# A chunked linear recurrence and two feed-forward layers on one core: other PSUM banks, score masks and state sums for the first attentions

## The chip, the cores and the metric

One core of one Trainium2 chip runs the whole kernel as a single launch. The time is device microseconds of one execution; the kernel before takes 1198.31 us (median of 3 runs, 1196.89 to 1199.21). The engines are named as the profile names them: PE (TensorE), with PEld for its weight loads, DVE (VectorE), ACT (ScalarE), POOL (GpSimd) and SP (the queue that starts most transfers).

## The reference, cut to what matters

A gated recurrence over 768 steps for 4 batches of 8 heads of width 48, with a complex decay per step, then two dense feed-forward layers on the 3072 resulting rows.

```python
def attention(q, k, v, a_re, a_im):             # B, H, S, D = 4, 8, 768, 48
    mag = sqrt(a_re**2 + a_im**2)
    scale = minimum(mag, 0.999) / (mag + 1e-6)
    ar, ai = a_re * scale, a_im * scale
    for t in range(S):
        S_re, S_im = ar[t] * S_re - ai[t] * S_im, ar[t] * S_im + ai[t] * S_re
        S_re = S_re + outer(k[t], v[t])
        y[t] = q[t] @ S_re

x = y as [3072, 384]
h = x @ w_in1;  x = (h * clip(h + 3, 0, 6) / 6) @ w_out1            # d_ff = 2048
h = x @ w_in2;  out = (max(h, 0) + alpha * min(h, 0)) @ w_out2
```

## The kernel before, in words

**Attention.** The 768 steps of a batch are cut into six chunks of 128 steps (C). A *group* n is two chunks of one batch, so there are 12 groups, three per batch. For each group VectorE and ScalarE norm the decays (`norm_ops`), and take their running products over the steps (`scan_ops`): local products over 8 steps, then totals of 16 blocks that PE transposes (`totals`, line 408, tile `ptt`), four doubling rounds, the *turn* that a chunk hands to the next (`phi`), and the products E, transposed back by PE (`back`, line 489, tile `pe`). From these come Kt and, in A, Qt (line 518): keys and queries with the decays folded in. `chunk_ops` is then the attention of one chunk g of the group. `tr` (line 563) transposes Kt and Qt by PE, four blocks at a time, into a PSUM tile `pt`, and ScalarE copies that to KT and QT. In the copy the output's access order puts neighbouring elements J = 8 elements apart. `scores(i)` makes 4 heads' scores in the PSUM tile `ps`, and VectorE multiplies them by the causal mask into PT (line 590). `outputs` (line 619) multiplies PT by v and, behind the first chunk, QT by the state W, into `py`; ScalarE copies `py` to ys, and six small transfers bring it into xr, the feed-forward's input. `update` (line 594) adds keys times values (`pu`) to W and scales W by the chunk's decay (`gx`). For groups below WACT = 4 the scaling is eight ScalarE instructions (line 614). KN, the keys in their natural order, comes by eight transfers per chunk.

**Feed-forward.** `ffn(layer, groups, ...)` runs one *pass*: layer 1 or 2 on one group (256 columns, a *single pass*) or on two groups (512 columns, a *pair pass*). Its 16 steps i have `ain` (9 products into `ph`), `gate` and `bout` (9 products into three accumulators `acc`). Every product of float32 numbers is three products of fp32r halves. The order of passes: layer 1 of group 0 (pass 0), layer 1 of group 1 (pass 1), layer 2 of both (pass 2), the same for groups 2 and 3, then pairs for the rest. `split_x` makes the halves xT of a group's input: a cast by ScalarE, a difference by VectorE.

**Weights.** They come as 64-bit floats. `decode_f64` and `split_w` turn a tile into two fp32r halves by four VectorE instructions, two of ScalarE and a difference on VectorE; that is done once per tile, in the passes that use it first, and the tiles stay in 15 places of SBUF or go out to a scratch buffer and come back.

**PSUM.** It has eight banks: two for `ph` (pool psh), one each for `pt` (also `ptt`, `pe`, `gx`), `ps` (also `pu`) and `py`, and three for acc0, acc1 and acc2.

**What sets the order.** A timeline gives each piece of work a position by hand (`group(...)` from line 732, `passes`), and pieces are issued in that order. A scheduler then orders each engine's queue by its own estimates and by priority, which falls in the order of issue. Each engine runs its queue strictly in order and waits at its head.

## Time and profile before

| what | value |
|---|---|
| median of 3 runs | 1198.31 us |
| the profiled execution | 1198.93 us |
| its span, from first to last instruction | 1197.2 us |
| busy PE, DVE, ACT, POOL | 1031.2, 802.1, 615.3, 2.0 us |
| mean granted TensorE clock | 0.975 |

The stages, by PE's rows: until 78 us norms, scan of group 0 and decoding of weights; attention 0 from 78.25 us; pass 0 at full rate from 121.61; attention 1 from 169.08; pass 1 from 210.67; pass 2 from 248.68 with attention 2 among its products; passes of layer 1 for groups 2 and 3 from 337.89 and 404.45, with attention 3 among the first; from 480 us pair passes of layers 1 and 2 in turn, each with the attention of later groups among its products.

How to read the rows: a group of instructions has its line, engine, operation, tiles (out<-in), forms and count, then its busy time and the mean time of one, then the idle time of the engine before them with the releaser. A wait names engine, tile and line on the left, and on the right what ended the wait. Times in windows are counted from the span's start.

### The profile page before, as it was taken

The page shows a single profiled execution, that of the slowest core. Times are in us where ns is not written, and L with a number is a line of the kernel's source. Part 1 is how long each engine was busy: PE and PEld are TensorE (multiplying, and loading weights), DVE is VectorE, ACT ScalarE, POOL GpSimd, SP SyncE. Part 2 cuts the span into 40 slices and gives each one's busy share as a digit, 9 for nine tenths or more (in the row PEclk, how much of TensorE's full clock was granted, in tenths as well). Part 3 has the DMA queues.
Part 4 walks back from the last instruction along what each step waited for, and adds up shares of the span by engine and source line. Part 5 has one row for each costly group of instructions (what it writes and reads, how often), then busy time and mean ns, then how long its engine had stood idle before and what let it go on. Part 6 is the DMA issues. An engine that isn't in the chain of part 4 may idle for free.

```text
span 1197.2 us, 15796 instructions
## 1 busy us (share of the span) xinstructions
PE 1031.2 (86%) x5914; PEld 846.9 (71%) x5914; DVE 802.1 (67%) x1537; ACT 615.3 (51%) x1003; POOL 2.0 (0%) x13
## 2 busy tenths in 40 slices
PE   0026946979998789999999999999999999999997
PEld 0015935957787787777878778778788777788786
DVE  7985973999895586948738749559579375333432
ACT  5453634667665455755356564446554346432433
POOL 0000000000000000000000000000000000000000
PEclk9999876999999899999999999999999999999999
DMA  8642472476575675445534544543454344244430
GB/s 339 253 167 61 142 303 67 134 275 194 222 247 181 213 243 178 134 128 174 171 102 153 171 120 158 193 136 116 131 188 139 130 124 138 89 163 134 133 129 30
DMA packets 70500, 194.60 MB, mean 163 GB/s; under 512 B 29456, under 2 KB 38672, under 8 KB 70416
## 3 DMA queue, kind: packets, MB, share of 16 engines
q1 hardware_dynamic: 70272, 193.50, 48.6%
q8 instruction: 49, 0.80, 0.3%
q14 instruction: 35, 0.29, 0.1%
q10 hardware_dynamic: 144, 0.01, 0.0%
HBM read 158.08 MB, written 22.81 MB: 151 GB/s over the span
## 4 chain that ended last, share of the span: by engine, by line
PE 66%; DVE 16%; ACT 12%; DMA 3%; issue 2%; SPq 0%; DVEq 0%; ACTq 0%
PE ph L658 27%; PE acc L695 24%; PE ps L589 5%; PE pt L566 4%; ACT KT L567 4%; ACT QT L567 4%; PE pu L599 3%; PE py L624 2%; DVE w L294 2%; DVE wd L76 2%; DVE wd L77 2%; PE py L626 2%; DMA w<-wsd 1%; DVE gs L680 1%; DMA A<-in_al_dram 1%
## 5 line engine op out<-in xcount | busy, mean ns | idle before, releaser
L695 PE MATMUL acc<-gs,w 128*128 128x512 f32 (+1 forms) x2016 | 453.3, 366 | 7.2 <-ACT gs L679 4.8
L695 PEld LDWEIGHTS acc<-gs,w 128*128 128x128 f32 x2016 | 335.2, 188 | 69.2 <-ACT gs L679 7.3
L658 PE MATMUL ph<-xT,w 128*128 128x256 f32 (+1 forms) x1152 | 231.2, 348 | 20.9 <-ACT xT L550 14.9
L658 PE MATMUL ph<-xs,w 128*128 128x512 f32 x864 | 224.3, 401 | 3.2 <-DVE xs L704 2.5
L658 PEld LDWEIGHTS ph<-xT,w 128*128 128x128 f32 x1152 | 185.1, 197 | 50.8 <-ACT xT L550 16.0
L658 PEld LDWEIGHTS ph<-xs,w 128*128 128x128 f32 x864 | 158.3, 188 | 40.6 <-DVE xs L704 4.0
L679 ACT CAST gs<-r 128x512 fp32r<-128x512 f32 x192 | 119.7, 624 | 119.6 <-DVE r L671 71.6
L680 DVE TENSOR_TENSOR gs<-r,gs 128x512 fp32r<-128x512 f32 x192 | 132.0, 689 | 63.5 <-ACT gs L679 63.4
L678 DVE SCALAR_TENSOR_TENSOR r<-n,nal,r 128x512 f32<-128x512 f32 x96 | 71.9, 749 | 80.9 <-ACT n L675 80.5
L670 ACT ACTIVATE r<-ph 128x512 f32<-128x512 f32 x96 | 57.3, 597 | 129.2 <-PE ph L658 128.7
L671 DVE SCALAR_TENSOR_TENSOR r<-r,ph 128x512 f32<-128x512 f32 x96 | 65.7, 684 | 83.4 <-ACT r L670 82.9
L674 ACT ACTIVATE r<-ph 128x512 f32<-128x512 f32 x96 | 57.5, 599 | 83.9 <-PE ph L658 83.1
L567 ACT COPY KT<-pt 96x512 f32<-96x512 f32 x48 | 54.8, 1143 | 47.6 <-PE pt L566 39.4
L590 DVE TENSOR_TENSOR PT<-ps,mask 128x512 f32<-128x512 f32 x48 | 33.2, 692 | 62.7 <-PE ps L589 61.0
L589 PEld LDWEIGHTS ps<-QT,KT 96*128 96x128 f32 x384 | 54.5, 214 | 21.8 <-ACT QT L567 18.5
L589 PE MATMUL ps<-QT,KT 96*128 96x128 f32 x384 | 60.5, 307 | 10.7 <-ACT QT L567 9.7
L567 ACT COPY QT<-pt 96x512 f32<-96x512 f32 x48 | 54.8, 1142 | 21.5 <-PE pt L566 21.5
L566 PE MATMUL pt<-ident,Kt 128*96 128x128 f32 x192 | 33.1, 298 | 38.0 <-DVE Kt L518 30.5
L675 ACT ACTIVATE n<-ph 128x512 f32<-128x512 f32 x96 | 57.4, 598 | 0.0
L566 PEld LDWEIGHTS pt<-ident,Kt 128*96 128x96 f32 x192 | 22.6, 136 | 48.6 <-ACT wd L73 21.2
L566 PE MATMUL pt<-ident,A 128*96 128x128 f32 x192 | 33.8, 303 | 20.9 <-ACT QT L567 10.3
L566 PEld LDWEIGHTS pt<-ident,A 128*96 128x96 f32 x192 | 20.9, 135 | 38.7 <-ACT QT L567 19.0
(107 smaller groups left out, 1054.0 us busy)
## 6 DMA issues: line engine op xcount, KB each, us to landing
w<-wsd SPq DMA_DIRECT2D x139, 768.0 KB, 4.4
raw<-in_w_dram SPq DMA_DIRECT2D x32, 768.0 KB, 5.7
wsd<-w SPq DMA_DIRECT2D x23, 768.0 KB, 4.1
A<-in_al_dram SPq DMA_DIRECT2D x12, 768.0 KB, 4.6
qk<-in_qkl_dram SPq DMA_DIRECT2D x12, 768.0 KB, 5.4
KN<-Kt SPq DMA_DIRECT2D x160, 48.0 KB, 2.3
v<-in_vl_dram SPq DMA_DIRECT2D x12, 384.0 KB, 4.4
out_dram<-o SPq DMA_DIRECT2D x18, 256.0 KB, 3.2
```

The source lines that it names most:

```text
L566: nc.tensor.transpose(pt[:D2, jj], src[:, 4 * half + jj, g].rearrange("p c d -> p (c d)"), ident)
L567: nc.scalar.copy(dst.rearrange("p h (t j) -> p j (h t)", j=J)[:, 4 * half : 4 * half + 4], pt[:D2])
L589: nc.tensor.matmul(ps[:, hh], lhsT=KTr[:, h], rhs=QT[:, h], start=True, stop=True)
L658: nc.tensor.matmul(ph_, lhsT=w[:, wl, kk], rhs=x[:, xl, kk], start=(kk == 0 and wl == 0 and xl == 0), stop=(kk == KT - 1 and wl == 1),)
L670: nc.scalar.activation(r, ph_, AF.Relu, bias=0.5, scale=1.0 / 6.0)
L671: nc.vector.scalar_tensor_tensor(r, r, 1.0, ph_, op0=ALU.min, op1=ALU.mult)
L674: nc.scalar.activation(r, ph_, AF.Relu)
L675: nc.scalar.activation(neg, ph_, AF.Relu, scale=-1.0)
L678: nc.vector.scalar_tensor_tensor(r[:, k], neg[:, k], nal[:, ii : ii + 1], r[:, k], op0=ALU.mult, op1=ALU.add)
L679: nc.scalar.copy(gs[:, 0], r)
L680: nc.vector.tensor_sub(gs[:, 1], r, gs[:, 0].bitcast(F32))
L695: nc.tensor.matmul(acc, lhsT=w[:, wl, e * P : (e + 1) * P], rhs=gs[:, gl], start=(i == 0 and wl == 0 and gl == 0), stop=(i == NF - 1 and g ...
```

## The change

- *Banks for the turn.* `totals` and `back` of groups 0 to 2 use the bank acc2 instead of `pt`. That bank is free because a single pass now has its three accumulators in two banks: one alone (acc1), two as halves of acc0. A product of zeros opens acc0, the two halves accumulate behind it, and their last step hands them on together.
- *Turns ahead.* `totals` and `back` of groups 0 to 3 are issued with a priority raised by 1000, so the scheduler puts them further ahead.
- *Banks for attentions 0 and 1.* Every second `pt` and the second `ps` of a chunk use a `ph` bank.
- *Copies of KT and QT, in all groups.* The copy now walks the output in runs of four neighbouring elements, and the PSUM input in steps of 128 elements.
- *Scores of groups 0 to 3.* ScalarE copies them to PT and GpSimd's affine_select zeroes what lies above the diagonal, in place.
- *State of groups 0 to 3.* W is added to `pu` by a product with the identity, and the eight scalings read PSUM. `gx` lies in the bank of `pu` in all groups.

```diff
+URGE = 1000
...
+    zero = cp.tile([1, P], F32R, tag="zero", name="zero")
+    nc.vector.tensor_scalar(zero, ident[0:1], 0.0, None, op0=ALU.mult)
...
+    def turn_bank(n, shape, name):
+
+        if n < 3:
+            return psf.tile(shape, F32, tag="acc2", name=name)
+        return ps1.tile(shape, F32, tag="pt", name=name)
...
+        def urgent(f):
+            def g():
+                with tc.high_priority(offset=URGE):
+                    f()
+            return g if n < 4 else f
...
-            pt = ps1.tile([P, 2, P], F32, tag="pt", name=f"ptt{n}")
+            pt = turn_bank(n, [P, 2, P], f"ptt{n}")
...
-        ops.append(totals)
+        ops.append(urgent(totals))
...
-            pe_ = ps1.tile([P, 2, G, 64], F32, tag="pt", name=f"pe{n}")
+            pe_ = turn_bank(n, [P, 2, G, 64], f"pe{n}")
...
-        ops.append(back)
+        ops.append(urgent(back))
...
+        def bank(k, own, name):
+
+            pool, tag = (psh, "ph") if n < 2 and k else (ps1, own)
+            return pool.tile([P, 4, P], F32, tag=tag, name=name)
+
         def tr(src, dst, half):
-            pt = ps1.tile([P, 4, P], F32, tag="pt", name=f"pt{n}_{g}_{half}")
+            pt = bank((src is Kt) == half, "pt", f"pt{n}_{g}_{half}")
             for jj in range(4):
                 nc.tensor.transpose(pt[:D2, jj], src[:, 4 * half + jj, g].rearrange("p c d -> p (c d)"), ident)
             nc.scalar.copy(
-                dst.rearrange("p h (t j) -> p j (h t)", j=J)[:, 4 * half : 4 * half + 4], pt[:D2]
+                dst.rearrange("p h (t j) -> p (h t) j", j=J)[:, :, 4 * half : 4 * half + 4],
+                pt[:D2].rearrange("p j x -> p x j"),
             )
 
...
-            ps = ps1.tile([P, 4, C], F32, tag="ps", name=f"ps{n}_{g}_{i}")
+            ps = bank(i, "ps", f"ps{n}_{g}_{i}")
...
-            nc.vector.tensor_mul(PT[i], ps, mask.unsqueeze(1).broadcast_to([P, 4, C]))
+            if n < WACT:
+                nc.scalar.copy(PT[i], ps)
+                nc.gpsimd.affine_select(
+                    PT[i], PT[i], pattern=[[0, 4], [1, C]], compare_op=ALU.is_ge, fill=0.0, base=0, channel_multiplier=-1
+                )
+            else:
+                nc.vector.tensor_mul(PT[i], ps, mask.unsqueeze(1).broadcast_to([P, 4, C]))
...
         def update():
             if c == NCH - 1:
                 return
-            pu = ps1.tile([P, H, D], F32, tag="ps", name=f"pu{n}_{g}")
+            pb = ps1.tile([P, H * D + H], F32, tag="ps", name=f"pu{n}_{g}")
+            pu, gx = pb[:, : H * D].rearrange("p (h d) -> p h d", d=D), pb[:, H * D :]
+            sums = n < WACT and c > 0
+            if sums:
+                nc.tensor.matmul(
+                    pu[:D2].rearrange("p h d -> p (h d)"), lhsT=ident[:D2, :D2],
+                    rhs=W_t[n, g].rearrange("p h d -> p (h d)"), start=True, stop=False,
+                )
             for h in range(H):
-                nc.tensor.matmul(pu[:D2, h], lhsT=KN[:, h], rhs=V[:, g, h], start=True, stop=True)
-            gx = ps1.tile([P, H], F32, tag="pt", name=f"gx{n}_{g}")
+                nc.tensor.matmul(
+                    pu[:D2, h], lhsT=KN[:, h], rhs=V[:, g, h], start=not sums, stop=not sums or h == H - 1
+                )
             nc.tensor.matmul(
                 gx[:D2], lhsT=sel[:, g].rearrange("p c d -> p (c d)"), rhs=gam_t[n], start=True, stop=True
             )
             W = lp.tile([D2, H, D], F32, tag="W", name=f"W{n}_{g}", bufs=2)
             gb = gx[:D2].unsqueeze(2).broadcast_to([D2, H, D])
-            if c == 0:
-                nc.scalar.copy(W, pu[:D2])
-            else:
-                nc.vector.tensor_add(W, W_t[n, g], pu[:D2])
             if n < WACT:
                 gs_ = lp.tile([D2, H], F32, tag="gsb", name=f"gsb{n}_{g}")
                 nc.scalar.copy(gs_, gx[:D2])
                 for h in range(H):
-                    nc.scalar.activation(W[:, h], W[:, h], AF.Copy, scale=gs_[:, h : h + 1])
+                    nc.scalar.activation(W[:, h], pu[:D2, h], AF.Copy, scale=gs_[:, h : h + 1])
             else:
+                if c == 0:
+                    nc.scalar.copy(W, pu[:D2])
+                else:
+                    nc.vector.tensor_add(W, W_t[n, g], pu[:D2])
...
         def bout(i, pos):
             gs = st.pop(("gs", i))
-            if i == 0:
-                st["acc"] = [psf.tile([P, 2 * GT], F32, tag=f"acc{e}", name=f"acc{layer}_{groups[0]}_{e}")[:, :N] for e in range(KT)]
+            if i == 0 and NP == 1:
+                st["acc"] = [psf.tile([P, N], F32, tag=f"acc{e}", name=f"acc{layer}_{groups[0]}_{e}") for e in range(KT)]
+            elif i == 0:
+                a2 = psf.tile([P, 2, N], F32, tag="acc0", name=f"acc{layer}_{groups[0]}_0")
+                a1 = psf.tile([P, N], F32, tag="acc1", name=f"acc{layer}_{groups[0]}_1")
+                nc.tensor.matmul(
+                    a2.rearrange("p a t -> p (a t)"), lhsT=zero, rhs=zero.unsqueeze(1).broadcast_to([1, 4, P]),
+                    start=True, stop=False,
+                )
+                st["acc"] = [a1, a2[:, 0], a2[:, 1]]
...
                 for wl, gl in ((0, 0), (1, 0), (0, 1)):
                     nc.tensor.matmul(
                         acc, lhsT=w[:, wl, e * P : (e + 1) * P], rhs=gs[:, gl],
-                        start=(i == 0 and wl == 0 and gl == 0), stop=(i == NF - 1 and gl == 1),
+                        start=(i == 0 and wl == 0 and gl == 0 and (NP == 1 or e == 0)),
+                        stop=(i == NF - 1 and gl == 1 and (NP == 1 or e != 1)),
                     )
...
+                if i == NF - 1:
+                    for ee in ((e,) if NP == 1 or e == 0 else () if e == 1 else (1, 2)):
+                        finish(ee)
```

In the rows below, names are those of the tiles with their numbers; in `pt_g_half`, `ps_g_i`, `py`, KT_g and so on the first number is the chunk of the group.

ScalarE, attention 0, first chunk and the start of the second, before:

```order
L567 COPY KT_0_248<-pt_0_0_265 96x4x128
L567 COPY KT_0_248<-pt_0_1_271 96x4x128
L567 COPY QT_0_247<-pt_0_0_277 96x4x128
L567 COPY QT_0_247<-pt_0_1_283 96x4x128
L612 COPY gsb_0_330<-gx_0_326 96x8
L567 COPY KT_1_253<-pt_1_0_348 96x4x128
L628 COPY ys_0_309<-py 128x512
L607 COPY W_0_328<-pu_0_317 96x384
L567 COPY KT_1_253<-pt_1_1_354 96x4x128
L614 ACTIVATE W_0_328<-W_0_328,gsb_0_330 96x48 x8
L567 COPY QT_1_252<-pt_1_0_362 96x4x128
L567 COPY QT_1_252<-pt_1_1_368 96x4x128
```

and now:

```order
L587 COPY KT_0_250<-pt_0_0_267 96x128x4
L587 COPY KT_0_250<-pt_0_1_273 96x128x4
L587 COPY QT_0_249<-pt_0_0_279 96x128x4
L587 COPY QT_0_249<-pt_0_1_285 96x128x4
L612 COPY PT_0_0_252<-ps_0_0_291 128x512
L612 COPY PT_0_1_253<-ps_0_1_298 128x512
L663 COPY ys_0_313<-py 128x512
L643 COPY gsb_0_332<-pu_0_321 96x8
L587 COPY KT_1_255<-pt_1_0_350 96x128x4
L645 ACTIVATE W_0_331<-pu_0_321,gsb_0_332 96x48 x8
L587 COPY KT_1_255<-pt_1_1_356 96x128x4
```

The two score copies stand ahead of the second chunk's KT, and the copy of `pu` to W is gone.

PE, attention 1 (the second chunk), before:

```order
L599 MATMUL pu_0_1173<-v_1048,KN_0_1097 96x48 x8
L566 MATMUL pt_1_1_1210<-ident,Kt_694 96x128 x4
L566 MATMUL pt_1_0_1216<-ident,A_360 96x128 x4
L566 MATMUL pt_1_1_1222<-ident,A_360 96x128 x4
L589 MATMUL ps_1_0_1228<-QT_1_1100,KT_1_1101 128x128 x4
L601 MATMUL gx_1_1273<-gam_689,sel 96x8
L412 MATMUL ptt_1732<-ident,tot 128x128 x2
L589 MATMUL ps_1_1_1234<-QT_1_1100,KT_1_1101 128x128 x4
L624 MATMUL py<-PT_1_0_1103,v_1048 48x128
L626 MATMUL py<-QT_1_1100,W_0_1184 48x128
```

and now:

```order
L586 MATMUL pt_1_0_1220<-ident,A_362 96x128 x4
L586 MATMUL pt_1_1_1226<-ident,A_362 96x128 x4
L427 MATMUL ptt_1737<-ident,tot 128x128 x2
L610 MATMUL ps_1_1_1239<-QT_1_1103,KT_1_1104 128x128 x4
L633 MATMUL pu_0_1178<-v_1051,KN_0_1100 96x48 x5
L507 MATMUL pe_1849<-ident,E_1620 128x128 x2
L633 MATMUL pu_0_1178<-v_1051,KN_0_1100 96x48 x3
L636 MATMUL pu_0_1178<-gam_692,sel 96x8
L610 MATMUL ps_1_0_1232<-QT_1_1103,KT_1_1104 128x128 x4
L628 MATMUL pu_1_1270<-W_0_1189,ident 96x384
L659 MATMUL py<-PT_1_0_1106,v_1051 48x128
L661 MATMUL py<-QT_1_1103,W_0_1189 48x128
```

`ptt` of group 2 has stayed in this attention and moved up two places, and `pe` of group 2, which stood in pass 1, stands among the products of state of this attention's first chunk.

VectorE, from Kt of group 1 on, before:

```order
L518 TENSOR_TENSOR Kt_694<-A_360,ts_693 128x1536
L398 TENSOR_TENSOR A_1349<-m_1611 128x2x48
L518 TENSOR_TENSOR A_360<-A_360,qk_677 128x1536
L396 TENSOR_TENSOR m_1611<-A_1349 128x384
L397 TENSOR_TENSOR A_1349<-m_1611 128x2x48
L398 TENSOR_TENSOR A_1349<-m_1611 128x2x48
L396 TENSOR_TENSOR m_1611<-A_1349 128x384
L397 TENSOR_TENSOR A_1349<-m_1611 128x2x48
L398 TENSOR_TENSOR A_1349<-m_1611 128x2x48
L590 TENSOR_TENSOR PT_0_0_1098<-ps_0_0_1137,mask 128x512
L590 TENSOR_TENSOR PT_0_1_1099<-ps_0_1_1143,mask 128x512
L609 TENSOR_TENSOR W_0_1184<-W_1_421,pu_0_1173 96x384
```

and now:

```order
L533 TENSOR_TENSOR Kt_697<-A_362,ts_696 128x1536
L722 TENSOR_TENSOR xs_1079<-acc_0_1_646,xs_1079 128x256
L533 TENSOR_TENSOR A_362<-A_362,qk_680 128x1536
L722 TENSOR_TENSOR xs_1079<-acc_0_0_645,xs_1079 128x256
L405 TENSOR_TENSOR m_1616<-A_1354 128x384
L722 TENSOR_TENSOR xs_1079<-acc_0_0_645,xs_1079 128x256
L406 TENSOR_TENSOR A_1354<-m_1616 128x2x48
L407 TENSOR_TENSOR A_1354<-m_1616 128x2x48
L405 TENSOR_TENSOR m_1616<-A_1354 128x384
L406 TENSOR_TENSOR A_1354<-m_1616 128x2x48
L407 TENSOR_TENSOR A_1354<-m_1616 128x2x48
L405 TENSOR_TENSOR m_1616<-A_1354 128x384
```

The score masks and the state sum are gone, and the local products of group 2 stand behind Kt of group 1, where before most of them stood ahead of it.

## Rows read from the trace of the kernel before

**Rows 1.** Windows by stage: busy us (x instructions), granted clock, DMA share, GB/s.
```profile
78.25:121.61 43.36, 27.61 (x152) 22.07 (x153) 24.72 (x59) 18.34 (x38) 0.00 (x0) 0.94 0.36 100
121.61:169.08 47.47, 36.27 (x288) 35.41 (x289) 45.24 (x85) 24.12 (x38) 0.00 (x0) 0.90 0.65 249
169.08:210.67 41.59, 26.34 (x170) 21.83 (x170) 15.45 (x48) 17.97 (x38) 0.00 (x0) 0.62 0.30 77
210.67:248.68 38.01, 35.51 (x286) 34.91 (x287) 36.04 (x52) 22.69 (x35) 0.00 (x0) 0.94 0.54 180
248.68:337.89 89.21, 80.89 (x421) 61.54 (x420) 82.23 (x134) 63.73 (x104) 0.00 (x0) 1.00 0.66 234
337.89:404.45 66.56, 55.27 (x461) 50.71 (x459) 45.61 (x109) 32.73 (x65) 0.00 (x0) 0.99 0.63 198
...
480.00:1197.20 717.20, 696.92 (x3607) 555.89 (x3605) 428.01 (x803) 354.77 (x572) 0.00 (x0) 1.00 0.43 137
```

**Rows 2.** Timeline of PE, attentions 0 and 1: start, us, instruction, idle before.
```profile
78.25 1.06 PE L566 MATMUL pt<-ident,Kt 128*96 128x128 f32 x4 [20.84 <-DVE Kt L518]
80.50 1.08 PE L566 MATMUL pt<-ident,Kt 128*96 128x128 f32 x4 [1.19 <-ACT KT L567]
...
120.35 0.80 PE L658 MATMUL ph<-xT,w 128*128 128x256 f32 x2 [5.43 <-ACT xT L550]
...
169.08 1.06 PE L566 MATMUL pt<-ident,Kt 128*96 128x128 f32 x4 [9.66 <-DVE Kt L518]
...
208.87 0.80 PE L658 MATMUL ph<-xT,w 128*128 128x256 f32 x2 [5.34 <-ACT xT L550]
```

**Rows 3.** Waits of PE from 240 us: us in total, times, longest.
```profile
PE pt L566 <- ACT KT L567: 9.0, 25, 0.5
PE ps L589 <- ACT QT L567: 5.0, 13, 0.5
PE acc L695 <- ACT gs L679: 4.6, 5, 1.6
PE pt L566 <- ACT QT L567: 4.4, 13, 0.5
PE ph L658 <- ACT xT L550: 4.2, 1, 4.2
PE ph L658 <- DVE xs L704: 2.5, 2, 1.3
PE ph L658 <- DVE xT L551: 2.2, 1, 2.2
```

**Rows 4.** Waits of PE from 480 us.
```profile
PE pt L566 <- ACT KT L567: 5.5, 16, 0.4
PE ps L589 <- ACT QT L567: 3.0, 8, 0.4
PE pt L566 <- ACT QT L567: 2.2, 7, 0.3
PE ptt L412 <- ACT KT L567: 1.1, 3, 0.4
```

**Rows 5.** Groups by line, ScalarE: forms, count | busy us, mean ns | idle before.
```profile
L567 ACT COPY KT<-pt 96x512 f32<-96x512 f32 x48 | 54.8, 1143 | 47.6 <-PE pt L566 39.4 <-PE ps L589 8.0
...
L628 ACT COPY ys<-py 128x512 f32<-128x512 f32 x24 | 14.1, 587 | 33.7 <-PE py L626 26.0 <-PE py L624 5.6 <-DMA w<-wsd 1.8
```

**Rows 6.** Waits of VectorE, 78.25 to 210.67 us.
```profile
DVE PT L590 <- PE ps L589: 31.6, 7, 8.0
DVE W L609 <- PE pu L599: 9.5, 3, 4.2
```

**Rows 7.** Groups by line, GpSimd.
```profile
L247 POOL TENSOR_SCALAR_AFFINE_SELECT mask<-mask 128x128 f32<-128x128 f32 x1 | 0.3, 295 | 0.0
```

**Rows 8.** Groups by line, PE: 512 fp32r columns, and 128 fp32 columns.
```profile
L695 PE MATMUL acc<-gs,w 128*128 128x512 f32 x1440 | 375.6, 401 | 3.9 <-ACT gs L679 3.7
...
L566 PE MATMUL pt<-ident,A 128*96 128x128 f32 x192 | 33.8, 303 | 20.9 <-ACT QT L567 10.3 <-ACT KT L567 9.6
```

More of the change, by code (lines that the diff above doesn't have):

```diff
@@ L680, in gate, with finish @@
             nc.vector.tensor_sub(gs[:, 1], r, gs[:, 0].bitcast(F32))
+        def finish(e):
+            acc = st["acc"][e]
+            if layer == 1:
+                xs = xs_t[m][:, :, e, cs]
+                nc.scalar.copy(xs[:, 0], acc)
+                nc.vector.tensor_sub(xs[:, 1], acc, xs[:, 0].bitcast(F32))
+            else:
+                o = st["o"][:, e, :N]
+                nc.scalar.copy(o, acc)
+                t0 = groups[0] * GT
+                nc.sync.dma_start(out[e * P : (e + 1) * P, t0 : t0 + N], o)
         def bout(i, pos):
             gs = st.pop(("gs", i))
-            if i == 0:
-                st["acc"] = [psf.tile([P, 2 * GT], F32, tag=f"acc{e}", name=f"acc{layer}_{groups[0]}_{e}")[:, :N] for e in range(KT)]
+            if i == 0 and NP == 1:
[8 more added lines that the diff above has]
+                st["acc"] = [a1, a2[:, 0], a2[:, 1]]
             if i == NF - 1:
```

11 lines of the change are left out of this document (removed).

## The prediction, made before the changed kernel was run

> **What bounds the kernel now.** I read the windows by stage first [rows 1]: PE is the engine to fill, and it is full only late. From 480 us on it is busy 696.92 of 717.20 us; between 78 and 211 us, where the first two attentions and the first single pass stand, it is busy 27.61 + 36.27 + 26.34 of 132.4 us, at a granted clock down to 0.62. So time is to be had in the front, where PE waits, and behind it only as far as PE still has gaps.
>
> Then PE's own rows [rows 2]. Attention 0 goes in single file: the first four transpositions start at 78.25, the next four at 80.50, 1.19 us after PE fell idle, released by ScalarE's copy of KT. There is one `pt` bank, so a step is transpositions (1.06) plus copy plus hand-overs, 2.25 us, and a chunk has four. At its end PE stands 5.43 us until xT of group 0 is there (score outputs, six small transfers, cast). Attention 1 does not start when pass 0 ends: PE waits 9.66 us for VectorE's Kt of group 1. Then the same file again, and 5.34 us for xT.
>
> Why Kt is late is in VectorE's waits [rows 6]: in these stages it stood 31.6 us ahead of score masks and 9.5 us ahead of state sums, at the head of its queue, waiting for PE. It did no scan and no weights meanwhile, and ran full in pass 0 (45.24 of 47.47 us [rows 1]).
>
> Last, PE's waits behind 240 us [rows 3] and behind 480 us [rows 4]: what is left there is mostly KT and QT, 18.4 us behind 240 with 10.7 of it behind 480, and 1.1 us where `ptt` waits for the bank of a KT copy.
>
> **The change part by part.** *The copies of KT and QT.* Now 1143 ns for 96x512, each element written 32 bytes behind the one before; the copy of `py`, as many elements from PSUM, read and written in a row, takes 587 ns [rows 5]. The step in the write is all that differs, so it costs 556 ns. The changed copy writes runs of four (16 bytes) and instead reads PSUM 512 bytes apart at each element. No row shows ScalarE reading PSUM so. Ends: 0.59 us if the reading step is free; 1.14 if it costs what the writing step did; 1.70 if it costs that on top of a dear write. I take 0.6: the one dear form in the trace is a single element per step on the writing side, and that is removed.
>
> [...]
>
> *Attention 0.* Its stage idles 43.36 − 27.61 = 15.7 us [rows 1], 5.4 of it for xT [rows 2]. The other 10.3 are the single file. With `ph` as a second bank, four transpositions (1.06) run while the copy before them does, so a chunk's four steps fall from 4 × 2.25 = 9.0 to some 4 × 1.06 + 0.6 = 4.9 us, and the second scores no longer wait for the first. What stays is one uncovered copy per chunk, 0.7 us. Masks move to ScalarE and GpSimd: a copy like that of `py`, 0.59, then an affine_select of 128x512. The nearest is 295 ns for 128x128 [rows 7]; bounds are 0.3 and 1.2 us, I take 0.9, since it grows with the elements. So a PT takes 1.5 us on two engines and a hand-over between; the products of state (`pu`), which PE's order puts ahead of them, cover it. In ScalarE's order the totals of group 1 stand behind both score copies, and PE's transposition of E stands ahead of pass 0: that chain lies beside the 5.4 us wait for xT and may outlast it by 0 to 3 us. Of the 10.3 stay 1.4 for the uncovered copies and 0.9 for E: **−8 us** (ends −10 and −4).
>
> *The wait for Kt of group 1.* VectorE's order has no mask and no state sum of the first groups in it, so the 31.6 + 9.5 us are free to it. The turn of group 1 is done before pass 0 (PE's `pe` of that group stands ahead of the pass instead of in its last third), and group 2's local products, which stood ahead of Kt, now stand behind it. Less than a quarter of the 41.1 us has to be usable to bring Kt forward by 9.66; in the stage of pass 0 that means 36 us of work in place of 45.24, beside a pass of some 38 (47.47 − 9.66). Kt is ready when the pass ends: **−9.7** (ends −9.7 and 0).
>
> *Attention 1.* It idles 41.59 − 26.34 = 15.2 us, 5.3 for xT, 9.9 in the file. These go, but a new wait comes: "turns ahead" puts `ptt` and `pe` of group 2 into this attention. PE's `pe` stands before the last three `pu` and the first scores of chunk 1, ScalarE's y, E and EL copies before gsb, the W scalings and the PT copies. All of it waits for VectorE to take group 2 from Kt to E. That is about the 15.45 us that it was busy in this stage: masks and sums are out, local products in. PE is there after less, some 13 us (half of its 26.34), and then the uncovered W scaling and masks follow, each of them another 2 to 3 us on ScalarE and GpSimd. I give back 8 of 9.9: **−2** (ends −9.9 and +3). What it buys is Kt of group 2 inside attention 1 instead of at the start of pass 2.
>
> *Pass 2 with attention 2 (248.68 to 337.89).* PE idles 8.3 us, VectorE is busy 82.23 of 89.21. [rows 3] name the gaps: gs 4.6, xs 2.5, the rest KT and QT. VectorE loses the eight masks of attentions 2 and 3 and the scan that came earlier. Half the idle goes: **−4** (ends 0 and −7).
>
> *KT and QT behind it.* 7.7 us between 240 and 480 [rows 3, 4]; about 1.2 lie in pass 2 above, so **−6**. Behind 480: 5.5 + 3.0 + 2.2 + 1.1 = 11.8 us; each single wait is at most 0.5 us and the copy gets 0.55 shorter: **−11**. PE is the bound there, so nothing is late next but PE itself. If the copy keeps its price, both terms are 0.
>
> *xT of group 3.* 4.2 + 2.2 us [rows 3]. PE's order ends attention 3 with 31 products of the pass behind it instead of 17: **−3** (0 to −5).
>
> *What is added on PE.* Five 96x384 identity products for the sums; three of the 128-column products of 303 ns are an upper end of 0.9 us each [rows 8], and only two stand where PE is full. Four products of zeros of 512 columns, 0.4 at most by the same rows, two of them in gaps. **+2.5**. GpSimd's hand-overs in attentions 2 and 3, among dense products: **+1** (0 to 3). The banks of the single passes and the later xs of thirds 1 and 2 cost nothing beside `pe` and attention work that now fills that place; uncovered they are 1 us.
>
> Sum: −8 −9.7 −2 −4 −6 −11 −3 +2.5 +1 = −40.2, against the profiled execution's 1198.93 us: 1158.7. The median lies 0.6 below that execution, so **1158 us**.
>
> **The rivals.** *A: the reading step costs what the writing step did.* For: no row reads PSUM so. Against: a free read would be in line with every contiguous row. The 6, the 11 and 1 us of pass 2 are lost, a copy of 1.14 is again longer than its transpositions (1.5 lost in attention 0, 1 in attention 1), and xT of group 3 gains 1 less: −18.7, **1180 us**.
>
> *B: the front's gain is eaten by queue order.* VectorE stays full through pass 0, or ScalarE's queue, in order behind y and EL of group 2, holds the PT copies. For: the order in attention 1. Against: 41 us of VectorE's waits removed. Then 10 of the 11.7 us of Kt and attention 1 go: **1168 us**.
>
> *C, slower: the new copy is dearer than the old.* 96 copies stand alone on PE's way, so each 0.1 us costs 9.6 us; rival A's −18.7 is used up when a copy takes 1.14 + 0.2 = 1.34 us. At 1.70: −18.7 + 54 = +35, **1233 us**. For it speaks only that no row excludes it.
>
> *D: the front shrinks further*, with attention 1 losing its whole 9.9 and pass 2 its 7 us: −51.1, **1147 us**.
>
> That the change does not do what it says is out for the order of instructions (masks, sums and banks are there in the order shown); for the copies it is rival A.
>
> **How the numbers follow.** Forecast 0.57, A 0.17, B 0.13, C 0.06, D 0.07. The range reaches from 1143 (D with the better ends of attention 0 and xT) to 1181 (A). It leaves out C, the worse half of A's bounds and the worst ends of the forecast. A difference of 0.2% (2.4 us) is about what a measurement of this kernel tells from none. Faster: all but C and a share of combined mishaps, 0.91; within 0.2%: 0.02; slower 0.07.
>
> **What would show it.** Right: the KT row at about 0.6 us; transpositions of attention 0 one behind another; pass 0 at full rate near 114 us, attention 1 near 151, pass 1 near 191, pass 2 near 229; no score mask among VectorE's waits before 240 us; KT and QT waits behind 480 us under 2 us. Wrong: a KT copy above 1 us, PE waiting over 5 us for Kt of group 1, or over 12 us for `pe` and PT in attention 1.

## The result, and the profile after

The changed kernel takes 1141.83 us (median of 4 runs, 1138.18 to 1145.18) against 1198.76 us of the kernel before beside it: ratio 0.9528 (95% interval 0.9503 to 0.9553). The forecast was faster at 1158 us, range 1143 to 1181: the direction is right, the time lies just below the range. The profiled execution took 1138.18 us, 60.75 less than the one before; it is the shortest of the four, 3.7 us under their median, so two kernels whose profiles are 3 or 4 us apart at a late mark are not told apart by that.

Windows by stage of the changed kernel (columns as in [rows 1]): attention 0, pass 0, attention 1, pass 1, from pass 2 to the first product of attention 4, and the rest.

```profile
78.10:114.84 36.74, 25.22 (x157) 20.70 (x157) 25.50 (x72) 16.41 (x43) 6.43 (x4) 0.91 0.44 119
114.84:152.80 37.96, 35.11 (x286) 34.73 (x286) 36.89 (x49) 22.16 (x34) 0.00 (x0) 0.96 0.58 219
152.80:192.34 39.54, 23.11 (x175) 18.63 (x175) 26.93 (x69) 16.94 (x43) 2.93 (x4) 0.75 0.51 169
192.34:229.38 37.04, 35.81 (x290) 35.12 (x290) 33.41 (x50) 22.57 (x35) 0.00 (x0) 0.94 0.64 206
229.38:404.35 174.97, 167.36 (x1133) 144.65 (x1133) 143.36 (x271) 109.07 (x205) 6.33 (x8) 0.99 0.68 234
404.35:1136.50 732.15, 725.84 (x3886) 589.43 (x3884) 455.12 (x874) 344.26 (x606) 0.00 (x0) 1.00 0.44 145
```

The last two stages in the kernel before, cut at the same events:

```profile
248.68:438.37 189.69, 168.72 (x1132) 144.08 (x1131) 154.87 (x289) 114.86 (x199) 0.00 (x0) 0.98 0.65 220
438.37:1197.20 758.83, 735.40 (x3886) 587.96 (x3884) 456.21 (x873) 376.91 (x606) 0.00 (x0) 1.00 0.43 140
```

Up to pass 2 the kernel is 19.3 us ahead (229.38 against 248.68; forecast 229). Pass 2 itself takes 81.05 us instead of the 89.21 of [rows 1], and TensorE is idle there for 1.9 us instead of 8.3:

```profile
229.38:310.43 81.05, 79.14 (x416) 62.22 (x417) 78.62 (x132) 61.48 (x109) 3.79 (x4) 1.00 0.70 250
```

From the start of pass 2 to attention 4 the kernel gains 14.7 us, and behind that 26.7. At the same 3886 products TensorE's busy time in that last stage falls by 9.6 us, beside 17.1 us of idle time: part of the gain never showed as a wait.

Timeline of TensorE in the changed kernel (answers to [rows 2]):

```profile
112.44 0.66 PE L507 MATMUL pe<-ident,E 128*128 128x128 f32 x2 [5.95 <-DVE E L499]
113.84 0.80 PE L693 MATMUL ph<-xT,w 128*128 128x256 f32 x2 [0.74 <-ACT xT L565]
...
152.80 1.08 PE L586 MATMUL pt<-ident,Kt 128*96 128x128 f32 x8 [2.13 <-DVE Kt L533]
...
171.75 0.66 PE L507 MATMUL pe<-ident,E 128*128 128x128 f32 x2 [4.60 <-DVE E L499]
...
175.44 2.07 PE L610 MATMUL ps<-QT,KT 96*128 96x128 f32 x8 [1.90 <-ACT W L645]
...
189.99 0.80 PE L693 MATMUL ph<-xT,w 128*128 128x256 f32 x2 [5.05 <-ACT xT L565]
```

The transpositions come eight in a row now: of a chunk's four `pt`, in the order of use, the second and the third lie in the two `ph` banks (not every second one), the first and the fourth in `pt`. The wait for Kt of group 1 is 2.13 us instead of 9.66; in attention 1 new waits for E and W stand in the file's place, as forecast.

Groups by line, ScalarE and GpSimd (answers to [rows 5, 7]), and TensorE's waits from 240 us (answers to [rows 3]):

```profile
L587 ACT COPY KT<-pt 96x512 f32<-96x512 f32 x48 | 28.0, 588 | 32.1 <-PE pt L586 31.9
L663 ACT COPY ys<-py 128x512 f32<-128x512 f32 x24 | 14.1, 586 | 33.1 <-PE py L661 23.0 <-PE py L659 9.9 <-DMA KN<-Kt 0.2
L612 ACT COPY PT<-ps 128x512 f32<-128x512 f32 x16 | 9.3, 587 | 14.0 <-PE ps L610 14.0
L613 POOL TENSOR_SCALAR_AFFINE_SELECT PT<-PT 128x512 f32<-128x512 f32 x16 | 15.7, 986 | 341.7 <-ACT PT L612 341.7
```

```profile
PE ph L693 <- DMA w<-wsd: 2.4, 5, 0.8
PE acc L736 <- DVE xs L722: 1.6, 1, 1.6
PE ph L693 <- DVE xT L566: 1.2, 1, 1.2
PE pe L507 <- DVE E L499: 0.4, 1, 0.4
PE ph L693 <- DVE r L706: 0.3, 1, 0.3
```

The KT copy takes 588 ns, as long as the copy of `py` (586 ns), which reads and writes in a row. From 240 us on no wait for KT or QT is listed any more, none for gs (the gate's output, 4.6 us before), and 1.2 us of 6.4 for xT. Those for xs (layer 1's result, which is layer 2's input) were 2.5 us in two waits. Now one of 1.6 stands where `acc` is opened for a single pass, and one of 0.8 ahead of 240 us.

### The profile page after: what moved, and what is told of

Its sections match the earlier page's. It is cut to its first block, busy times and chain, and to the rows that moved or that the text cites. A ratio compares the mean times of both kernels' runs of the same rounds, so it can differ in the third digit from the quotient of the medians.

```text
span 1136.5 us, 15843 instructions
## 1 busy us (share of the span) xinstructions
PE 1014.6 (89%) x5928; PEld 844.2 (74%) x5928; DVE 790.8 (70%) x1517; ACT 571.9 (50%) x1017; POOL 17.7 (2%) x29
## 4 chain that ended last, share of the span: by engine, by line
PE 78%; DVE 13%; DMA 3%; ACT 3%; issue 1%; SPq 1%; POOL 1%; ACTq 0%; DVEq 0%
PE ph L693 33%; PE acc L750 31%; PE ps L610 4%; PE pt L586 3%; PE pu L633 2%; PE py L659 2%; PE py L661 1%; DMA w<-wsd 1%; DVE w L297 1%; DVE wd L77 1%; DVE wd L78 1%; DMA raw<-in_w_dram 1%; DVE wd L75 1%; DVE m L405 1%; DVE A L381 1%
## 5 line engine op out<-in xcount | busy, mean ns | idle before, releaser
L610 PEld LDWEIGHTS ps<-QT,KT 96*128 96x128 f32 x384 | 50.1, 200 | 13.7 <-ACT QT L587 7.4
L610 PE MATMUL ps<-QT,KT 96*128 96x128 f32 x384 | 55.5, 291 | 4.8 <-ACT QT L587 2.9
L586 PE MATMUL pt<-ident,Kt 128*96 128x128 f32 x192 | 30.5, 287 | 22.9 <-DVE Kt L533 22.9
L405 DVE TENSOR_TENSOR m<-A 128x384 f32<-128x384 f32 x84 | 46.8, 557 | 2.0
L659 PE MATMUL py<-PT,v 128*48 128x128 f32 x384 | 41.7, 293 | 2.9 <-POOL PT L613 2.7
L587 ACT COPY KT<-pt 96x512 f32<-96x512 f32 x48 | 28.0, 588 | 32.1 <-PE pt L586 31.9
L523 DVE TENSOR_TENSOR Ts<-A,EL 128x1536 f32<-128x1536 f32 x24 | 42.1, 1754 | 1.4 <-ACT EL L510 1.3
L74 ACT ACTIVATE wd<-raw 128x768 f32<-128x768 f32 x32 | 29.2, 912 | 19.2 <-DVE w L297 15.3
```

What stands on the lines that cost most here:

```text
L405: ops.append((0.55, lambda: V.tensor_mul(m.rearrange("p g a c d -> p g a (c d)"), x, y)))
L586: nc.tensor.transpose(pt[:D2, jj], src[:, 4 * half + jj, g].rearrange("p c d -> p (c d)"), ident)
L610: nc.tensor.matmul(ps[:, hh], lhsT=KTr[:, h], rhs=QT[:, h], start=True, stop=True)
L659: nc.tensor.matmul(o, lhsT=V[:, g, h], rhs=PT[h // 4][:, h % 4], start=True, stop=(c == 0))
```

## The experiments

"Copy" below is the change's new KT and QT copy. Attention 4's first product is the mark between front and rest.

### The copy: alone, undone, and late only

```diff
# copy_alone: kernel before, all groups; copy_late: n >= 4 only
-dst.rearrange("p h (t j) -> p j (h t)", j=J)[:, 4 * half : 4 * half + 4], pt[:D2]
+dst.rearrange("p h (t j) -> p (h t) j", j=J)[:, :, 4 * half : 4 * half + 4],
+pt[:D2].rearrange("p j x -> p x j"),
# copy_undone: changed kernel, the same lines the other way
```

> The kernel before with the new form of the KT and QT copy everywhere and nothing else of the change. Theory 1 (a stop of TensorE at a copy costs the idle time that the waits show and about 0.17 us of lost overlap between products, and a shorter ScalarE queue also ends waits for gs): behind the start of pass 2 the 54 stops at KT and QT show 19.6 us, with 54 x 0.17 = 9.2 us beside them and some 5 us of gs and xT waits, so -34 us there, and -8 to -12 us ahead of it (attention 0 and 1): 1155 us (1148 to 1165). Theory 2 (only the idle time that the waits show, as the prediction counted): -19.6 us behind, -8 us ahead: 1171 us. Theory 3 (the gain comes from the banks and the masks, the copy is worth little): above 1180 us.

> The changed kernel with the old form of the KT and QT copy. Theory 1 (visible wait and lost overlap): 28.5 us of stops come back behind the start of pass 2, some 5 us of gs waits, and 3 to 10 us in the attentions ahead of it, where two banks take turns now: 1180 us (1173 to 1187). Theory 2 (visible waits only): +18 to +20 us: 1162 us. Theory 3 (the copy is worth little): under 1152 us.

> The kernel before with the new copy form in the attentions of groups 4 to 11 alone; the 42 stops of TensorE at KT and QT there show 14.9 us of idle time in the profile of the kernel before, and nothing else of those stages changes. Theory 1 (each stop costs 0.17 us of lost overlap beside what the wait shows): -14.9 - 42 x 0.17 = -22 us, 1177 us, with the busy time of TensorE down by some 7 us at the same count of products. Theory 2 (visible waits only): -15 us, 1184 us, with the busy time unchanged. These lie 7 us apart, over twice the spread of the runs.

Measured: copy_alone 1156.23 us, ratio 0.9665 (0.9633 to 0.9696), 41.8 us faster than before; copy_undone 1178.22 us (0.984, 0.9815 to 0.9866), 36.4 us slower than the change; copy_late 1172.90 us (0.9791, 0.9767 to 0.9815), 25.1 us faster than before. Theory 1's times hold for the first two, theory 2's in none; copy_late gained 3 us more than theory 1 said. The copy is about two thirds of the change, by itself (41.8 of 56.9 us) and as the last part added (36.4).

In copy_undone the old form is dear again, 1158 ns beside 1143 in the kernel before, though the rest of the change stands around it:

```profile
L587 ACT COPY KT<-pt 96x512 f32<-96x512 f32 x48 | 55.0, 1158 | 32.0 <-PE pt L586 31.9
```

copy_late is the clean case. TensorE's waits behind 438.37 us in the kernel before:

```profile
PE pt L566 <- ACT KT L567: 6.9, 20, 0.5
PE ps L589 <- ACT QT L567: 3.9, 10, 0.5
PE pt L566 <- ACT QT L567: 3.0, 9, 0.5
PE ptt L412 <- ACT KT L567: 1.1, 3, 0.4
```

and that stage in copy_late:

```profile
438.26:1170.70 732.44, 725.60 (x3886) 589.66 (x3884) 454.20 (x873) 343.96 (x606) 0.00 (x0) 1.00 0.45 145
```

The waits removed are 42 and show 14.9 us; the stage is 26.4 us shorter, 9.8 of it in busy time. What a stop costs beside its wait is seen at a place that has the same products with and without it, four of `acc` and then the scores. Timeline of TensorE, before:

```profile
607.97 1.18 PE L695 MATMUL acc<-gs,w 128*128 128x512 f32 x4
609.58 1.16 PE L589 MATMUL ps<-QT,KT 96*128 96x128 f32 x8 [0.42 <-ACT QT L567]
```

and in the changed kernel:

```profile
564.52 1.18 PE L750 MATMUL acc<-gs,w 128*128 128x512 f32 x4
565.54 1.16 PE L610 MATMUL ps<-QT,KT 96*128 96x128 f32 x8
```

From start to start it is 1.61 us with the stop and 1.02 without: 0.59 us, of which the wait shows 0.42. Without a stop the scores start 0.16 us before the last `acc` ends (as the profile models its end); that overlap is lost. At `ptt` and the next `pt` behind it the same comparison gives 0.52 for 0.35 shown and 0.47 for 0.31. From attention 4 on, the traces of the kernel before and of copy_late have the same products (3884 starts) in the same order, so they can be compared start by start. The 42 stops cost 21.2 us, 0.50 each: 14.9 shown and 6.3 of lost overlap. Twelve more stops at KT and QT, of 0.08 to 0.14 us of idle time each, are too short for the list of waits and cost 3.2 us, 0.24 to 0.31 each. The last 2.0 of the 26.4 us are spread over the other products and the end.

### Masks and sums back on VectorE

```diff
# masks_vector, changed kernel
-            if n < WACT:
+            if n < 0:
                 nc.scalar.copy(PT[i], ps)
# masks_sums_vector: that, and
-            sums = n < WACT and c > 0
+            sums = False
...
+                if c == 0: nc.scalar.copy(W, pu[:D2])
+                else: nc.vector.tensor_add(W, W_t[n, g], pu[:D2])
-                    nc.scalar.activation(W[:, h], pu[:D2, h], AF.Copy, ...)
+                    nc.scalar.activation(W[:, h], W[:, h], AF.Copy, ...)
```

> The changed kernel with the score masks of groups 0 to 3 by VectorE again (a multiply out of PSUM, no copy and no GpSimd); banks, order, copy and PSUM sums stay. Theory 1 (VectorE's queue, stopped at each mask, holds back the work that makes Kt of group 1, as the prediction said): TensorE's wait for that Kt grows from 2.1 us by some 5 to 10 us, 1150 us (1146 to 1156). Rival (with two banks and the turns ahead the scores come early enough, and GpSimd's 986 ns a mask costs TensorE as much as VectorE's queue did): within 3 us of the changed kernel, 1139 to 1145 us.

> The changed kernel with both the score masks and the state sums of groups 0 to 3 by VectorE again; banks, turns ahead and copy stay. Theory of the prediction, what is left of it after masks_vector (VectorE's queue has to be free of waits for PE so that Kt of group 1 comes in time; the sums alone were 9.5 of 41.1 us): TensorE's wait for that Kt grows by 5 to 10 us, 1148 to 1152 us. Rival (the turn of group 1 ahead of pass 0 brings Kt forward, whoever does masks and sums): attention 1 still starts within 2 us of 152.8, 1140 to 1146 us.

Measured: 1140.83 us (0.9517, 0.9496 to 0.9538) and 1141.98 us (0.9523, 0.9506 to 0.9540), both the same as the change. Attention 1 starts at 152.25 and 152.30 us. The rival won twice: the parts on which the prediction rested the 9.7 us for Kt bring nothing that can be measured, as long as banks and turn stand. (What they do without the turn is seen in scores_only below.)

### Turn, order and banks undone one by one

```diff
# no_urge: priorities as before          # no_turn: that, and the bank pt again
-            return g if n < 4 else f
+            return f
-        if n < 3:
+        if n < 0:
# no_banks: attentions 0 and 1 with one bank each for pt and ps
-            pool, tag = (psh, "ph") if n < 2 and k else (ps1, own)
+            pool, tag = (psh, "ph") if False and k else (ps1, own)
```

> The changed kernel without the raised priority of totals and back, and with their tiles in the bank pt again; the rest stays. Theory (the turn ahead, not the freed VectorE, brings Kt of group 1 forward): attention 1 starts 6 to 10 us later than at 152.8, and Kt of group 2 inside pass 2 again: 1150 us (1147 to 1156). Rival (VectorE's freed queue brings it): attention 1 within 2 us of 152.8, 1140 to 1145 us.

> The changed kernel with one bank each for pt and ps in attentions 0 and 1; the rest stays. Theory of the prediction (with a copy of 0.59 us a step of the single file is 1.06 + 0.59 + hand-overs of some 0.1 us against 1.06 with two banks, eight such steps in each attention, less the one that stays uncovered): 0.6 x 6 = 3.6 us in attention 0 and up to as much in attention 1, 1147 us (1144 to 1150). Rival (attention 0 and 1 end on other chains, E, masks and xT, and the banks give nothing): 1140 to 1143 us.

> The changed kernel without the raised priority of totals and back, their tiles in acc2 as in the change. It tells which half of the turn matters: if the order does, this is as slow as the kernel without both (theory: 1150 us, attention 1 later by 6 to 10 us); if the bank does, it is within 3 us of the changed kernel. I lean to the order, since with the bank alone the instructions stand where the scheduler had them.

Measured: no_turn 1146.26 us (0.9573, 0.9547 to 0.9599), no_banks 1146.92 (0.9585, 0.9562 to 0.9608), no_urge 1147.35 (0.9572, 0.9550 to 0.9593): each 4 to 6 us slower by the medians, with intervals that overlap that of the change or nearly do. The times lie near what the first theories gave, but for no_turn and no_urge not their reason: attention 1 still starts at 153.1, 151.4 and 152.9 us. So no single one of these parts is needed to bring Kt of group 1 forward; the losses come behind it (pass 1 at full rate at 193.1, 200.3 and 195.8 us against 192.3, and attention 4 at 409.8, 410.6 and 413.1 against 404.4).

### Each part by itself, with the copy

```diff
# turn_only: masks_sums_vector + no_banks
# scores_only: no_turn + no_banks
# banks_only: masks_sums_vector + no_turn
# split_masks, changed kernel
-            if n < WACT:
+            if n < WACT and i == 1:
                 nc.scalar.copy(PT[i], ps)
```

All four keep the copy, single passes in two banks, and `gx` in the bank of `pu`.

> Copy in the new form and the turn ahead (raised priority and acc2, single passes in two banks); score masks and state sums of groups 0 to 3 by VectorE, one bank each for pt and ps. Theory (masks off VectorE, turn ahead and banks each bring Kt of group 1 forward by themselves, so that undoing one costs little): attention 1 starts within 2 us of 152.8, and the time is that without the banks, 1147 us (1144 to 1150). Rival (VectorE has to be rid of masks and sums, or PE has to have the second banks): attention 1 starts at 157 us or later, as with the copy alone (162), 1151 to 1156 us.

> Copy in the new form, scores by ScalarE and GpSimd and sums in PSUM; no turn ahead and one bank each for pt and ps. Theory (each part brings Kt of group 1 forward by itself): attention 1 starts within 3 us of 152.8, 1149 us (1146 to 1153), the losses of no_turn and no_banks together being at most 10 us. Rival (the freed VectorE gives nothing): attention 1 at 158 to 162 us, 1154 to 1157 us, as with the copy alone.

> Copy in the new form and the second banks of pt and ps in attentions 0 and 1; masks and sums by VectorE, no turn ahead. Theory (each part by itself): attention 1 starts within 3 us of 152.8, 1147 us (1144 to 1151). Rival (banks shorten only the single file of attention 0 and 1 and do nothing for Kt): attention 1 at 157 to 159 us with TensorE waiting 5 us or more for Kt, 1150 to 1154 us.

> The changed kernel with the first score mask of each chunk of groups 0 to 3 by VectorE out of PSUM and the second by ScalarE and GpSimd, so that neither runs two in a row. If the masks stand on the way at all (TensorE waits 2.4 us for GpSimd's PT in attention 0), 1138 to 1140 us, better than both forms; if they do not, as masks_vector says, 1140 to 1143 us.

Measured: turn_only 1145.89 us (0.9570, 0.9549 to 0.9590), scores_only 1153.33 (0.9620, 0.9593 to 0.9647), banks_only 1140.72 (0.9527, 0.9496 to 0.9558), split_masks 1138.45 (0.9510, 0.9486 to 0.9535). turn_only did what its theory said, in time and in place (attention 1 at 153.0 us). banks_only is as fast as the whole change, though Kt came at 156.8 us and neither theory gave that time. scores_only is near the copy alone, 2.9 us faster: freeing VectorE hardly helps the time by itself. split_masks is the lowest median of all, but its interval overlaps the change's, so it isn't told apart from it.

Freeing VectorE does help Kt. Where TensorE transposes E of group 1, a step on the way to that Kt, tells how long it then waits. scores_only, with VectorE freed and priorities as before, has it ahead of pass 0:

```profile
117.15 0.66 PE L507 MATMUL pe<-ident,E 128*128 128x128 f32 x2 [2.59 <-DVE E L499]
...
156.89 0.65 PE L586 MATMUL pt<-ident,Kt 128*96 128x128 f32 x4 [0.28 <-DVE Kt L533]
```

turn_only, with masks and sums on VectorE and the raised priority, has it 2 us into pass 0:

```profile
118.33 0.66 PE L507 MATMUL pe<-ident,E 128*128 128x128 f32 x2
...
152.96 0.64 PE L586 MATMUL pt<-ident,Kt 128*96 128x128 f32 x4 [1.65 <-DVE Kt L533]
```

In all kernels with E of group 1 ahead of pass 0 or in its first 5 us, the wait for Kt is 0.3 to 5.0 us, also when a wait for xs just ahead of it is added. In those that have it 25 us or more into the pass (before, copy_alone, copy_late and, below, plain_banks, second_pt, second_ps and plain_split) it is 7.8 to 9.7 us; in banks_only it is 5.1, and 8.3 with the one for xs. So either the freed VectorE or the raised priority moves that step, which is why undoing one of them shows nothing. scores_only loses it again in attention 1: 52.1 us up to the first product of pass 1, against 36.3 with the copy alone, 5.3 of them a wait for E of group 2.

VectorE's waits between 78 and 210 us show how it came to wait for masks. copy_alone:

```profile
DVE PT L591 <- PE ps L590: 21.7, 7, 6.2
DVE W L610 <- PE pu L600: 9.2, 3, 4.0
```

banks_only:

```profile
DVE PT L617 <- PE ps L610: 9.0, 7, 2.6
DVE W L647 <- ACT gsb L643: 4.8, 1, 4.8
```

[rows 6] had 31.6 us for PT. The same masks on the same engine wait 21.7 with the short copy and 9.0 in banks_only (13.4 in plain_banks below, which has the second banks alone): VectorE waited because TensorE went in single file, and making the file shorter frees VectorE of most of that wait without taking the masks away.

### Only the banks, then the order

```diff
# plain_banks: kernel before + copy + bank() of the change for pt and ps
# second_pt, second_ps: plain_banks with the one or the other alone
# plain_split: plain_banks + split masks
# banks_urge: plain_banks +
-        ops.append(totals)
+        ops.append(urgent(totals))
-        ops.append(back)
+        ops.append(urgent(back))
```

> The kernel before with two edits alone: the new form of the KT and QT copy, and the second banks of pt and ps in attentions 0 and 1. Masks, sums, gx, priorities and the three accumulator banks of the single passes are as before. Theory (copy and second banks are the whole gain; VectorE's waits for masks were TensorE's single file seen from the other side): 1141 us (1138 to 1145), VectorE's waits for PT between 78 and 210 us about 9 us, the first product of attention 4 between 404 and 410 us. Rival (the single passes' two banks or gx in the bank of pu are needed as well): 1146 to 1153 us, attention 4 at 412 to 420 us.

> The kernel before with the new copy form and the second bank of pt alone in attentions 0 and 1. If the single file of the transpositions is what counts (eight steps in each attention), nearly all of the banks' gain over the copy alone (1156 us) is here: 1141 to 1145 us. If the file of scores and masks counts as much, about half: 1147 to 1151 us.

> The kernel before with the new copy form and the second bank of ps alone in attentions 0 and 1. If the transpositions' file is what counts: 1153 to 1156 us, hardly better than the copy alone. If scores that wait for VectorE's mask of the ones before count as much: 1147 to 1151 us, and VectorE's waits for PT between 78 and 210 us fall from 21.7 to about 12 us.

> plain_banks with the second score mask of each chunk of groups 0 to 3 by ScalarE and GpSimd. If split masks take 2 us off, as between the changed kernel and split_masks (1141.8 and 1138.45 us, within each other's spread): 1138 to 1140 us; if that was spread, the same as plain_banks within 2 us.

> The kernel before with the new copy form, the second banks of pt and ps in attentions 0 and 1 (plain_banks, 1156 us) and the raised priority of totals and back; no other bank, mask or sum is changed. In plain_banks the transposition of E of group 2 stands in pass 1 (at 227 us) and attention 2 begins at 270; here the order has it ahead of pass 1. Theory (the place of group 2's turn decides whether the banks pay): attention 4 at 405 to 411 us, 1139 to 1146 us. Rival (the accumulator banks or gx in the bank of pu are what was missing): attention 4 at 416 to 421 us, 1152 to 1157 us.

Measured: plain_banks 1156.03 us (0.9650, 0.9626 to 0.9675), second_pt 1147.92 (0.9581, 0.9557 to 0.9604), second_ps 1167.23 (0.9737, 0.9720 to 0.9753), plain_split 1147.67 (0.9601, 0.9559 to 0.9643), banks_urge 1145.40 (0.9548, 0.9523 to 0.9572).

My theory for plain_banks fell, and so did its rival: the second banks gave nothing over the copy alone. second_pt has part of the gain, short of the 1141 to 1145 us expected if the transpositions' file were all, and the second `ps` bank alone cost 11 us, which neither theory gave. What differs is where the scheduler puts the turn of group 2. In plain_banks one half of E is transposed at the start of pass 1 and the other far inside it:

```profile
197.80 0.27 PE L492 MATMUL pe<-ident,E 128*128 128x128 f32 x1
...
227.11 0.27 PE L492 MATMUL pe<-ident,E 128*128 128x128 f32 x1
```

In banks_urge, which differs from it by the priority alone, both stand ahead of pass 1:

```profile
184.61 0.66 PE L498 MATMUL pe<-ident,E 128*128 128x128 f32 x2 [3.27 <-DVE E L490]
```

Attention 2 then begins at 219.2 us instead of 270.6, and the time falls by 10.6 us, into the theory's range (attention 4 at 412.8 us lies between the two forecasts).

Where plain_banks loses can be read from its trace. It reaches pass 2 at 229.07 us, 9.0 ahead of copy_alone (238.10), and attention 4 only 0.9 ahead; the stretch between takes 190.9 us against 182.8:

```profile
229.07:420.00 190.93, 169.50 (x1132) 146.76 (x1131) 159.90 (x283) 110.93 (x203) 0.00 (x0) 0.95 0.64 222
238.10:420.90 182.80, 167.60 (x1132) 144.70 (x1131) 154.34 (x289) 107.57 (x199) 0.00 (x0) 0.98 0.68 228
```

TensorE's longest wait there is one for gs, at the second `acc` step of pass 2; with the copy alone all its waits for gs in that stretch are 2.9 us:

```profile
253.36 4.22 PE L700 MATMUL acc<-gs,w 128*128 128x512 f32 x9 [7.98 <-ACT gs L684]
```

ScalarE makes gs from VectorE's r, and from 242.7 to 251.9 us VectorE's queue has weights and products of group 2's decays (tile `Ts`) ahead of that r, with no gap:

```profile
248.91 1.75 DVE L508 TENSOR_TENSOR Ts<-A,EL 128x1536 f32<-128x1536 f32 x1
...
251.92 0.74 DVE L683 SCALAR_TENSOR_TENSOR r<-n,nal,r 128x512 f32<-128x512 f32 x1
```

In banks_urge VectorE makes both `Ts` at the start of pass 1 (186.3 and 189.1 us, against 235.8 and 248.9), and the longest wait for gs between pass 2 and attention 4 is 2.8 us:

```profile
186.28 1.75 DVE L514 TENSOR_TENSOR Ts<-A,EL 128x1536 f32<-128x1536 f32 x1
```

In second_pt the transposition of E stands at 217.5 us and in second_ps, which has such a wait of 5.6 us, at 240.0; in every kernel of this study that is faster than second_pt it stands ahead of pass 1. plain_split has it at 186.4 us, 2 us ahead of pass 1, and its median is 8.4 us below that of plain_banks, four times what split masks were to give; this fits the place of the turn better than a price of masks, but one of its four runs took 1156.4 us, and the intervals overlap. It is not the whole rule: scores_only has it at 186.8 us, ahead of pass 1, and is slow, with pass 1 beginning only at 209.0. And banks_only is 15.3 us faster than plain_banks with the priorities as before; the two differ by the two banks of the single passes (with their later xs) and by `gx`, and no run separates those.

### VectorE's work taken away

```diff
# no_clamp, changed kernel: layer 2 tiles
-    V.tensor_scalar(t, t, W_MIN, W_MAX, op0=ALU.max, op1=ALU.min)
+    if clamp:
+        V.tensor_scalar(t, t, W_MIN, W_MAX, op0=ALU.max, op1=ALU.min)
```

> The changed kernel without the clamp of the magnitude in the decoding of the 16 weight tiles of layer 2 (that part of the computation is left out): 16 VectorE instructions of 577 ns, 9.2 us, and nothing on TensorE. Theory (from 215 to 335 us VectorE is busy 116.9 of 120 us, and the front ends when it is through with its work, so work taken off it comes off the time nearly one for one): the first product of attention 4 at 395 to 399 us instead of 404.4, and 1134 us (1131 to 1137). Rival (TensorE's own chain or the transfers of weights bind the front, VectorE being full is only its backlog): attention 4 within 2 us of 404.4, 1139 to 1144 us.

Measured: 1143.95 us (0.9546, 0.9518 to 0.9575), the same as the change; attention 4 at 409.0 us. My theory fell; the time is the rival's, the place of attention 4 neither's. Windows of the changed kernel:

```profile
78.10:215.00 136.90, 106.09 (x798) 96.72 (x799) 108.61 (x214) 69.02 (x141) 9.35 (x8) 0.88 0.51 167
215.00:335.00 120.00, 115.76 (x703) 96.42 (x701) 116.91 (x206) 82.36 (x142) 3.79 (x4) 1.00 0.70 244
```

and of no_clamp:

```profile
78.10:215.00 136.90, 105.84 (x722) 94.87 (x723) 100.31 (x200) 65.81 (x136) 9.46 (x8) 0.79 0.48 156
215.00:335.00 120.00, 116.84 (x714) 97.92 (x713) 115.88 (x196) 83.00 (x143) 3.60 (x4) 1.00 0.68 241
```

VectorE did 8.3 us less ahead of 215 us and was as full as before behind it, but TensorE is 96 to 97% busy there too, and shows 3 to 4 us of idle time to win. The test isn't pure: the scheduler put other work in the room, and Kt of group 1 came 4 us later (156.9 us).

### Where all kernels differ

| kernel | attention 1 | first xT product of pass 1 | E of group 2 | attention 4 | from there to the end |
|---|---|---|---|---|---|
| before | 169.1 | 208.9 | 209.6 | 438.4 | 758.8 |
| copy_undone | 157.9 | 199.0 | 180.6 | 420.5 | 755.6 |
| copy_late | 169.2 | 208.9 | 209.7 | 438.3 | 732.4 |
| copy_alone | 162.1 | 198.4 | 199.2 | 420.9 | 733.1 |
| plain_banks | 157.2 | 190.4 | 197.8, 227.1 | 420.0 | 732.5 |
| banks_urge | 154.6 | 185.4 | 184.6 | 412.8 | 732.9 |
| no_turn | 153.1 | 192.0 | 173.3 | 409.8 | 732.7 |
| banks_only | 156.8 | 184.9 | 181.6 | 407.0 | 733.2 |
| after | 152.8 | 190.0 | 171.8 | 404.4 | 732.2 |

Behind attention 4 every kernel with the new copy there takes 732 to 734 us, whatever stands ahead. So the change is two sums: 26.7 us there, which copy_late shows to be the copy, and 34.0 us ahead, of which the copy alone brings 17.5.

## Why the prediction was right and wrong

- **Price of the copy**: 0.6 us taken, 0.588 measured. Rivals A and C are out: 588 ns with a reading step of 512 bytes, 586 in a row (the copy of `py`). The 588 ns are for runs of four elements written; with single elements written 32 bytes apart, and the reading in a row, it was 1158 (copy_undone).
- **Attention 0** (-8): full rate of pass 0 at 114.84 us, 6.8 earlier, between the ends. The wait for E took 5.95 us, but 4.7 of it lies where xT had been waited for.
- **Kt of group 1** (-9.7): 7.5 us of the 9.66 went, and the stage of pass 0 is 9.5 us shorter. The size held, and so did one link of the reason, the turn of group 1 done by the start of pass 0. That VectorE has to be freed of masks and sums for it did not hold: freed, it moves that turn (scores_only), but the raised priority does the same without (turn_only, masks_sums_vector).
- **Attention 1** (-2): 39.54 us for 41.59, -2.05. What it gives back is E 4.6, W 1.9 and PT 0.7 us. The granted clock of the stage is 0.75, against 0.62.
- **Pass 2, xT of group 3, KT and QT up to attention 4**: the first failed step, *"Half the idle goes: −4"*. With xT (-3), some -3.5 of the KT and QT term and +3 of added work, about -7.5 was forecast between pass 2 and attention 4; it was 14.7. Pass 2 alone gave 8.2, past the end of -7: its idle time fell from 8.3 to 1.9 us, not by half but by three quarters, and its busy time by 1.8. In the whole stretch the listed waits for gs went from 3.7 us to none, for xT from 6.4 to 1.2, for KT and QT from 4.7 to 0.7; for xs from 2.5 only to 2.4, and the added work is not seen (busy time fell by 1.4). With the copy alone the stretch takes 182.8 us, 6.9 less than before; the other 7.8 us come with the turn, the banks and the masks together, and these are not separated.
- **KT and QT behind it**: the second failed step, *"each single wait is at most 0.5 us and the copy gets 0.55 shorter: −11"*. Right mechanism, wrong size: with the rest of the term for 240 to 480 us and +0.5 of added work, about -13 was forecast from attention 4 on; the change gained 26.7 there, and the copy by itself 26.4 (copy_late). The prediction took the listed idle time for the price of a stop. The 42 listed stops showed 0.36 us each and cost 0.50, and the list leaves out twelve shorter ones. Rival C of the prediction had the other price, each copy in full: 96 copies at 0.55 us would be 53 us, and the copy alone gained 41.8.

The two steps miss about 7 and 14 us, the front up to pass 2 less than 1; together that is the 20.5 us between 1158.7 and the profiled 1138.18 (16 us between the forecast and the median). The signs that were to show the forecast right all came, the times of the stages up to pass 2 within 2 us, so none of them could tell that the part behind was mis-sized. Rival D's time was nearest: of its two halves, pass 2 losing its 7 us came, attention 1 losing its whole file did not. Rival B didn't come.

What stays open: that the place of group 2's turn decides whether the second banks pay is shown by one pair of runs and fits the others, but the raised priority moves the turns of other groups too, and no run moves group 2's alone. What the single passes' two banks and the place of `gx` bring is not separated either.

## What to carry to other kernels

Where an engine that is full stops for the same short reason dozens of times, price a stop by the distance from start to start of the same instructions with and without it, not by the idle time that the wait shows, and count the stops that are too short for the list; here a stop cost 0.50 us for 0.36 shown. A wait of one engine for another at the head of its queue says who was late, not which work to move: here shortening the file of the late one (banks_only) gave more than taking work off the waiting one (scores_only). Where two parts each do the same thing, undoing one shows nothing: that does not tell that neither does it. And a part that pays or costs by where the scheduler then puts something else has to be run with and without its neighbours: undone one by one, the parts beside the copy looked worth 0 to 6 us each, and the runs that have the copy and few of them lie anywhere from 11 us behind the copy alone (second_ps) to 15 ahead (banks_only).
